# w_in's middle columns loaded in row halves of 512 columns, with eight blocks of the first tile computed in two halves

## The chip, the cores and the metric

The kernel runs on one core of a Trainium2 chip. A core has TensorE (PE, matrix products), VectorE (DVE), ScalarE (ACT), GpSimd (POOL) and the SyncE queue (SP), each with its own instruction stream; they wait for each other through semaphores. SP and POOL also issue DMAs. The metric is the device time of one execution in microseconds, lower is better. The time before is 282.33 us (median of 3 runs, 281.98 to 282.49).

## The reference, cut to what matters

Linear attention feeds a two-layer network with a snake activation.

```python
q_s = softmax over head_dim of q           # (8, 8, 576, 64)
k_s = softmax over the sequence of k
kv  = einsum('bhsd,bhse->bhde', k_s, v)
x   = einsum('bhsd,bhde->bhse', q_s, kv)   # reshaped to (4608, 512)
h   = x @ w_in                             # w_in: 512 x 2048, float32
s   = sin(alpha * h)
g   = h + s * s / (alpha + 1e-9)
out = g @ w_out                            # w_out: 2048 x 512
```

## The kernel before, in words

The 4608 tokens are cut into nine tiles of 512. For each tile the 2048 columns of h are cut into 16 blocks of 128. One block of one tile is a sum of four matmuls (`mm_h`, L275), one for each chunk of 128 rows of w_in, in the order `KO = (0, 2, 1, 3)` of chunks; `mm_h(t, ni, k0, k1)` does only the steps k0 to k1 of the four, so that a block can be begun at one place and finished at another. Steps 0 and 1 read chunks 0 and 2 of w_in and of x, steps 2 and 3 chunks 1 and 3.

A block ni of tile t then goes through `sine` (L286): ScalarE takes sin(alpha * h) from PSUM into a buffer s (four buffers), and s is squared on VectorE (D), POOL (P) or ScalarE (A) by a string of letters; for tile 0 it is `"DPPAPPAPPAAPPAPD"`. `combine` (L297) on VectorE adds h, still in PSUM, to the scaled square, and writes g. Only with that is the PSUM bank free. Which bank a block of tile 0 gets is written out (L266): `0: "aabbkllaabbkllaa"`, where a, b and l have two banks each and k (tile name kvp) has one. So block 11 takes the bank of block 4, blocks 7 and 8 those of 0 and 1, 9 and 10 those of 2 and 3, 12 and 13 those of 5 and 6.

The order of every engine's instructions is written out by hand. Tile 0 (L415 to L483): while the attention of batch 0 gives x in two steps (chunks 0 and 2 first, then 1 and 3), blocks 0 to 3 get their first two steps (L421, L428). Then `h_slot` (L431) runs for ni = 0 to 15: `mm_h` (from step 2 for the first four blocks, from step 0 for the others), then the sine, then the combine of the block before. Between them stand, in `late` (L476): after block 6 and after block 12 a copy on VectorE that lets SP load parts of q, k and v of batch 1, and after blocks 8 and 10 POOL's issues of w_out's rows 8 to 13. POOL's stand in its queue behind the squares of the blocks before them.

After tile 0 `o_quad` (L439) computes the output product of tile 0 in four accumulators at once, in the banks b, b, l, l (L485): first w_out's row blocks 0 to 3, then 4 to 7, 8 to 11 and 12 to 15. Between its steps stands the attention of batch 1 (L515 to L552): exponentials on ScalarE, sums and norm on VectorE, transposes and products on TensorE. From then on the tiles follow one another, h of one tile interleaved with the output product of the tile before.

w_in and w_out are float32 in DRAM and bf16 on the chip. The loads cast, and POOL issues them (L358 to L365): the columns 0 to 511 in three transfers by chunks, then four pieces of 256 columns with all four chunks (128x4x256, rows of 512 bytes on the chip), then the last quarter, columns 1536 to 2047, in one transfer (rows of 1024 bytes), then w_out's row blocks 0 to 3 and 4 to 7. SP's loads of q, k and v share the same 16 DMA engines.

Of the kernel before, what the change touches and what calls it, by code (L numbers as in the profile page):

```python
# [23 lines left out]
def kernel(  # L24
# [82 lines left out]
    def load_win(c0, c1, cc=slice(0, 4)):  # L107
        nc.gpsimd.dma_start(out=win[:, cc, c0:c1], in_=win_v[:, cc, c0:c1])  # L108
# [159 lines left out]
    def bank(kind):  # L268

        if kind == "k":  # L270
            return ps_k.tile([128, 2, MF], F32, name="kvp", tag="a")[:, 0]
        pool = {"a": lambda: ps_h[0], "b": lambda: ps_h[1], "l": lambda: ps_l, "o": lambda: ps_o[0], "p": lambda: ps_o[1]}[kind]()
        return pool.tile([128, MF], F32, name={"l": "lp", "o": "op", "p": "op"}.get(kind, "hp"), tag=kind)

    def mm_h(t, ni, k0=0, k1=4):  # L275

        if ni == 0 and k0 == 0:
            G[t] = gpool.tile([128, nN, MF], BF16, name="g")
        hp = HP[t, ni] if k0 else bank(BANKS.get(t, 3 * "aabb" + "abba")[ni])
        HP[t, ni] = hp  # L280
        for k in range(k0, k1):
            nc.tensor.matmul(hp, win[:, KO[k], ni * 128:(ni + 1) * 128],  # L282
                             xT[:, KO[k], t * MF % NX:t * MF % NX + MF], start=(k == 0), stop=(k == 3))
        return hp

    def sine(t, ni, hp, sq):  # L286
        s = spool.tile([128, MF], F32, name="s")
        nc.scalar.activation(s, hp, AX.Sin, scale=alpha_sb[:, ni:ni + 1])  # L288
        if sq == "A":
            nc.scalar.activation(s, s, AX.Square)  # L290
        elif sq == "P":
            nc.gpsimd.tensor_tensor(s, s, s, op=ALU.mult)  # L292
        else:
            nc.vector.tensor_tensor(s, s, s, op=ALU.mult)
        return s
# [62 lines left out]
    for c in range(2):  # L358
        load_win(256 * c, 256 * c + 256, slice(0, 4, 2))
    load_win(0, 512, slice(1, 4, 2))  # L360
    for c in range(2, 6):
        load_win(256 * c, 256 * c + 256)
    load_win(1536, 2048)
    for c in range(2):
        load_wout(4 * c, 4 * c + 4)  # L365
# [63 lines left out]
        mm_h(0, ni, ki, ki + 1)  # L429

    def h_slot(t, ni, sq, lag):  # L431
        hp = mm_h(t, ni, 2 if ni < (4, 2, 0)[min(t, 2)] else 0)
        lag.append((t, ni, hp, sine(t, ni, hp, sq)))

    def flush(lag, keep):
        while len(lag) > keep:
            combine(*lag.pop(0))
# [21 lines left out]
    with ES:  # L459
        def load_q1(ii):  # L460
            if ii == 0:
                staged["q", 1] = stage.tile([128, 4, J, D], F32, name="st_q", tag="st")
            st = staged["q", 1]
            DVE_CP(st[:, ii, 0, 0:1], zero)
            nc.sync.dma_start(out=st[:, ii::2, 0:8].rearrange("p i j d -> p i (j d)"),
                              in_=src_view(q, 1)[:, ii::2, 0:8 * D])

        def load_kv1():
            for n in "kv":
                staged[n, 1] = stage.tile([128, 4, J, D], F32, name=f"st_{n}", tag="st")  # L470
            for n, t, ii, j0, j1 in (("k", k, 0, 0, J), ("v", v, 0, 0, J), ("k", k, 1, 0, J),
                                     ("v", v, 1, 0, 5), ("v", v, 1, 5, J)):
                nc.sync.dma_start(out=staged[n, 1][:, ii::2, j0:j1].rearrange("p i j d -> p i (j d)"),
                                  in_=src_view(t, 1)[:, ii::2, j0 * D:j1 * D])

        late = {6: lambda: load_q1(0), 8: lambda: load_wout(8, 12), 10: lambda: load_wout(12, 14),  # L476
                12: lambda: (load_q1(1), load_kv1())}
        for ni in range(nN):
            h_slot(0, ni, "DPPAPPAPPAAPPAPD"[ni], lag)
            flush(lag, 1)  # L480
            if ni in late:
                late[ni]()
# [95 lines left out]
        for ni in range(nN):  # L578
            h_slot(1, ni, SQ[ni], lag)
            flush(lag, 1)  # L580
            if ni == 6:
                scale_q8()
            late_q8(ni)
# [69 lines left out]
    for ni in range(nN):  # L653
        h_slot(2, ni, SQ2[ni], lag)
        flush(lag, 2)
        if ni == 5:
            attn_kv(3)
        elif ni in (9, 13):
            ii = ni // 12
            x_copy(DVE_CP, slice(ii, 4, 2), 3, x_pair(3, ii))  # L660
    flush(lag, 0)

    for t in range(3, nT):
# [11 lines left out]
        for ni in range(nN):  # L675
            hp = mm_h(t, ni)
# [62 lines left out]
```

## Time and profile before

| what | us |
|---|---|
| median of 3 runs | 282.33 (281.98 to 282.49) |
| the profiled execution | 283.14 |
| its span | 281.3 |
| TensorE busy | 268.4 (95%) |
| ScalarE busy | 224.2 (80%) |
| VectorE busy | 187.1 (67%) |
| POOL busy | 80.2 (28%) |
| TensorE's mean granted clock, share of full | 0.999 |

Times in the profile are microseconds from the span's start. A matmul of 512 columns shows as 379 ns, but the next one starts before it ends, so TensorE's progress is read from the starts. The transfers of w_in landed at these times, read from the issue's start and the time to landing: columns 0 to 511 at 12.63, 13.30 and 15.53, the four pieces at 17.24, 18.52, 19.85 and 21.19, the last quarter at 24.50; w_out's row blocks 0 to 3 at 27.31, 4 to 7 at 31.07, 8 to 11 at 35.35, 12 and 13 at 38.29. Of batch 1, q landed at 29.78 and 34.91, and the parts of k and v at 37.73, 39.39, 40.83, 41.72 and 42.40.

### The profile page before, as it was taken

Reading aid. Unit: us, or ns where it says so; the run is one execution under the profiler, and the core shown is the slowest. Engines: PE = TensorE matmul, PEld = TensorE weight load, DVE = VectorE, ACT = ScalarE, POOL = GpSimd, SP = SyncE. Lnnn points to the kernel's source line nnn. Section 1 sums busy time; section 2 is a strip of 40 time slices with the busy share of each in tenths; the row PEclk is TensorE's granted clock in tenths of the full one; section 3 lists DMA queues with packets and bytes.
Section 4 is the critical chain, followed back from the end, with each engine's and each line's share of the span. In section 5 each row is a group of like instructions: output and inputs, shape, how many; then the busy total and the mean of one; then the engine's idle time right before and its main releaser. Section 6 shows DMA issues by size and latency. Waiting matters only on the chain.

```text
span 281.3 us, 4775 instructions
## 1 busy us (share of the span) xinstructions
PE 268.4 (95%) x1814; PEld 124.2 (44%) x1843; DVE 187.1 (67%) x279; ACT 224.2 (80%) x321; POOL 80.2 (28%) x75
## 2 busy tenths in 40 slices
PE   3899999999999999999999999999999999999994
PEld 1434454444444444444444444444444444444443
DVE  2968867999878767766776677577775555555422
ACT  4799457999588999899989998999877777777400
POOL 2959112678667450215011500350000000000000
PEclk9999999999999999999999999999999999999999
DMA  7999999795699039811981199125011111111143
GB/s 258 299 185 224 276 385 401 266 356 198 156 245 379 3 76 294 336 37 43 328 332 37 40 267 384 37 51 123 10 30 37 37 40 37 38 42 44 41 100 75
DMA packets 39607, 46.06 MB, mean 164 GB/s; under 512 B 17040, under 2 KB 22944, under 8 KB 39584
## 3 DMA queue, kind: packets, MB, share of 16 engines
q1 hardware_dynamic: 33952, 41.11, 46.1%
q0 software_dynamic: 5472, 4.52, 9.8%
q8 instruction: 14, 0.23, 0.3%
q10 hardware_dynamic: 160, 0.13, 0.2%
q14 instruction: 9, 0.07, 0.1%
HBM read 36.71 MB, written 9.44 MB: 164 GB/s over the span
## 4 chain that ended last, share of the span: by engine, by line
PE 87%; DMA 8%; POOL 2%; issue 1%; ACT 0%; SPq 0%; DVE 0%
PE hp L282 38%; PE op L302 37%; DMA wout<-in_moe_w_out_dram 4%; PE hp L302 2%; DMA win<-in_moe_w_in_dram 2%; PE lp L282 2%; DMA st_k<-in_k_dram 2%; PE kvp L173 2%; PE lp L302 1%; PE op L282 1%; PE op L709 1%; PE hp L237 1%; POOL s L292 1%; PE xp L237 1%; PE kvp L282 1%
## 5 line engine op out<-in xcount | busy, mean ns | idle before, releaser
L298 DVE SCALAR_TENSOR_TENSOR g<-s,inva_sb,hp 128x512 bf16<-128x512 f32 x129 | 95.1, 745 | 58.9 <-ACT s L290 53.3
L282 PE MATMUL hp<-xT,win 128*128 128x512 bf16 x508 | 128.8, 379 | 0.8 <-DMA win<-in_moe_w_in_dram 0.4
L302 PE MATMUL op<-wout,g 128*128 128x512 bf16 x463 | 117.6, 379 | 1.7 <-issue 1.3
L288 ACT ACTIVATE s<-hp,alpha_sb 128x512 f32<-128x512 f32 x129 | 87.0, 684 | 21.8 <-PE hp L282 20.3
L282 PEld LDWEIGHTS <-win 128*128 128x128 bf16 x576 | 55.6, 98 | 68.4 <-DMA win<-in_moe_w_in_dram 1.8
L302 PEld LDWEIGHTS <-g 128*128 128x128 bf16 x560 | 53.4, 98 | 65.4 <-issue 2.9
L290 ACT ACTIVATE s<-s 128x512 f32<-128x512 f32 x112 | 70.7, 632 | 3.6
L292 POOL TENSOR_TENSOR s<-s 128x512 f32<-128x512 f32 x28 | 29.5, 1066 | 17.8 <-ACT s L288 17.7
L152 POOL TENSOR_TENSOR qn<-qe,qs 128x1152 bf16<-128x1152 bf16 x11 | 23.2, 2128 | 30.7 <-DVE qs L146 26.3
L314 DVE COPY o<-op 128x512 f32<-128x512 f32 (+2 forms) x32 | 21.1, 660 | 9.7 <-PE op L302 7.4
L137 POOL CAST vb<-st_v 128x1152 bf16<-128x1152 f32 x12 | 14.4, 1228 | 44.5 <-DMA st_v<-in_v_dram 44.2
L118 ACT ACTIVATE qe<-st_q 128x1152 bf16<-128x1152 f32 (+2 forms) x18 | 17.7, 1026 | 6.3 <-DMA st_q<-in_q_dram 6.1
L118 ACT ACTIVATE ke<-st_k 128x1152 bf16<-128x1152 f32 x16 | 17.9, 1153 | 2.6 <-DMA st_k<-in_k_dram 2.6
L145 DVE TENSOR_REDUCE qs<-qe 128x36 f32<-128x2304 bf16 x5 | 12.8, 2552 | 8.3 <-ACT qe L118 8.3
L302 PE MATMUL hp<-wout,g 128*128 128x512 bf16 x45 | 12.0, 379 | 0.5 <-DMA wout<-in_moe_w_out_dram 0.3
L118 ACT ACT_TABLE_LOAD x7 | 9.0, 1283 | 0.8 <-PEq L723 0.7
L302 PE MATMUL lp<-wout,g 128*128 128x512 bf16 x32 | 9.2, 379 | 0.1
L369 PE MATMUL warm<-st_q,ident 128*128 128x512 f32 (+1 forms) x6 | 4.1, 806 | 4.7 <-DMA st_q<-in_q_dram 4.7
L282 PE MATMUL lp<-xT,win 128*128 128x512 bf16 x32 | 7.7, 379 | 0.4 <-DMA win<-in_moe_w_in_dram 0.4
L250 DVE CAST xT<-xp 128x1024 bf16<-128x1024 f32 (+1 forms) x7 | 7.4, 1065 | 0.0
L298 DVE SCALAR_TENSOR_TENSOR g<-s,inva_sb,lp 128x512 bf16<-128x512 f32 x8 | 5.7, 739 | 0.4 <-POOL s L292 0.4
L108 POOL DMA_DIRECT2D win<-in_moe_w_in_dram x8 | 5.9, 772 | 0.0
(98 smaller groups left out, 137.2 us busy)
## 6 DMA issues: line engine op xcount, KB each, us to landing
out_dram<-o SPq DMA_DIRECT2D x70, 128.0 KB, 2.3
st_q<-in_q_dram SPq DMA_DIRECT2D x6, 1152.0 KB, 6.3
st_k<-in_k_dram SPq DMA_DIRECT2D x6, 1152.0 KB, 9.1
st_v<-in_v_dram SPq DMA_DIRECT2D x6, 1152.0 KB, 11.3
st_k<-in_k_dram SPq DMA_DIRECT2D x4, 576.0 KB, 8.3
st_q<-in_q_dram SPq DMA_DIRECT2D x4, 512.0 KB, 6.2
wout<-in_moe_w_out_dram POOLq DMA_DIRECT2D x3, 512.0 KB, 13.7
win<-in_moe_w_in_dram POOLq DMA_DIRECT2D x5, 256.0 KB, 7.9
```

Source lines behind the costliest of these rows:

```text
L118: nc.scalar.activation(dst[:, :, ii * 128:(ii + 1) * 128].rearrange("p j (x d) -> p x j d", x=2), src[:, ii::2], AX.Exp)
L137: engs[ii](vv[:, 2 * ii:2 * ii + 2, :, 0:D], staged["v", b][:, ii::2])
L145: nc.vector.tensor_reduce(qs, A["qe", b].rearrange("p j (i d) -> p j i d", i=4), axis=AXL.X, op=ALU.add)
L152: engs[ii % len(engs)].tensor_tensor(qn[:, ii, 0:j1].rearrange("p j (x d) -> p j x d", x=2), qe[:, ii], part.unsqueeze(3).to_broadcast([12 ...
L250: eng(xT[:, c, d0:d0 + m - n], xp[..., n:m])
L282: nc.tensor.matmul(hp, win[:, KO[k], ni * 128:(ni + 1) * 128], xT[:, KO[k], t * MF % NX:t * MF % NX + MF], start=(k == 0), stop=(k == 3))
L288: nc.scalar.activation(s, hp, AX.Sin, scale=alpha_sb[:, ni:ni + 1])
L290: nc.scalar.activation(s, s, AX.Square)
L292: nc.gpsimd.tensor_tensor(s, s, s, op=ALU.mult)
L298: nc.vector.scalar_tensor_tensor(G[t][:, ni], in0=s, scalar=inva_sb[:, ni:ni + 1], in1=hp, op0=ALU.mult, op1=ALU.add)
L302: nc.tensor.matmul(acc, G[t][:, ni, j * 128:(j + 1) * 128], wout[:, ni, :], start=(ni == 0), stop=(ni == nN - 1))
L314: eng(o[:, cols], acc)
```

## The change

Columns 512 to 1535 of w_in come in four transfers as before, but each brings 512 columns of two chunks: first chunks 0 and 2 of columns 512 to 1023, then chunks 1 and 3 of them, then the same for columns 1024 to 1535. Rows on the chip are 1024 bytes per transfer instead of 512. In tile 0, ahead of block 4 the first two steps of blocks 4 to 7 are done, and ahead of block 8 those of blocks 8 to 11; `h_slot` then does only steps 2 and 3 of the blocks 4 to 11. Everything else stays in its order: on TensorE only these matmuls change places, POOL has four DMA issues of another shape, the other engines have the same instructions in the same order.

```diff
-    for c in range(2, 6):
-        load_win(256 * c, 256 * c + 256)
+    for c in (512, 1024):
+        for r in range(2):
+            load_win(c, c + 512, slice(r, 4, 2))
     load_win(1536, 2048)
...
     def h_slot(t, ni, sq, lag):
-        hp = mm_h(t, ni, 2 if ni < (4, 2, 0)[min(t, 2)] else 0)
+        hp = mm_h(t, ni, 2 if ni < (12, 2, 0)[min(t, 2)] else 0)
         lag.append((t, ni, hp, sine(t, ni, hp, sq)))
...
         for ni in range(nN):
+            for n in range(ni, ni + 4) if ni in (4, 8) else ():
+                mm_h(0, n, 0, 2)
             h_slot(0, ni, "DPPAPPAPPAAPPAPD"[ni], lag)
```

## The prediction

> **What bounds the kernel now.** I read the chain that ended last first, in order of time, because the change lies in the first tenth of the span and only the chain tells whether that tenth decides the end.
>
> ```profile
> 9.20 6.33 DMA win<-in_moe_w_in_dram
> 15.53 0.05 issue
> 15.57 1.90 PE hp L282 x8
> 17.48 0.86 PE kvp L282 x4
> 18.34 1.73 PE lp L282 x8
> 20.07 1.74 PE hp L282 x8
> 21.81 0.68 ACT s L288
> 22.56 1.98 POOL s L292 x2
> 24.54 10.81 DMA wout<-in_moe_w_out_dram
> 35.39 0.38 PE hp L302
> ```
>
> Columns: start, length, what. PE waits for w_in until 15.53, then two engines (ACT, POOL) lead to the issue of w_out's rows 8 to 11, which land at 35.35; from 35.39 on the chain is TensorE with issue gaps, to the end. So whatever moves TensorE's position at 35.39 moves the end one for one, as long as nothing later becomes late. Next, TensorE's timeline (start, length, what, idle before and its releaser):
>
> ```profile
> 15.57 1.90 PE L282 MATMUL hp<-xT,win 128*128 128x512 bf16 x8 [0.36 <-DMA win<-in_moe_w_in_dram]
> 17.31 1.03 PE L282 MATMUL kvp<-xT,win 128*128 128x512 bf16 x4
> 19.90 3.62 PE L282 MATMUL hp<-xT,win 128*128 128x512 bf16 x16
> 24.55 1.90 PE L282 MATMUL lp<-xT,win 128*128 128x512 bf16 x8 [0.39 <-DMA win<-in_moe_w_in_dram]
> 28.02 1.89 PE L302 MATMUL hp<-wout,g 128*128 128x512 bf16 x8
> 29.74 1.89 PE L302 MATMUL lp<-wout,g 128*128 128x512 bf16 x8
> 35.39 0.38 PE L302 MATMUL hp<-wout,g 128*128 128x512 bf16 x1 [0.30 <-DMA wout<-in_moe_w_out_dram]
> ```
>
> One matmul starts every 0.216 us ((3.62 - 0.38)/15). Between 15.57 and 35.39 TensorE stands twice: 0.39 before block 12 (w_in's last quarter) and 0.30 for w_out, 0.69 in all. That is the most that this change can win. The pieces of 256 columns are never waited for beyond hundredths: block 4 starts at 17.31.
>
> The ScalarE timeline in the same stretch shows no gap over 0.04 us between 16.28 and 29.10, 12.8 us for 16 sines (0.57 from one to the next) and 5 squares; so a late sine there is never made up. Last, the transfers: the software queue alone, first in the 512-byte packets of the pieces (17 to 19 us), then in the 1024-byte packets of the last quarter and w_out (21.2 to 24).
>
> ```profile
> DMA packets 787, 0.39 MB, mean 195 GB/s; under 512 B 25, under 2 KB 787, under 8 KB 787
> ...
> DMA packets 570, 0.57 MB, mean 203 GB/s; under 512 B 15, under 2 KB 570, under 8 KB 570
> ```
>
> **The change, part by part.**
>
> *POOL's issues.* Four transfers of 256 KB become four of 256 KB. The issue of the 128x2x512 shape took 0.74 (L108 at 9.20), that of 128x4x256 0.79: 4 x 0.05 = 0.2 us earlier for the last quarter and w_out's first halves. Both wait in the queue for some 10 us before they land, and POOL's next work is at 17.63 after an idle 2.48. Worth nothing.
>
> *The transfers.* 1,048,576 bytes at 195 GB/s are 5.38 us, at 203 GB/s 5.17. So the four land about 1.29 apart, at 17.2, 18.5, 19.8 and 21.1, the last quarter at 24.3 (24.50 before), w_out 8 to 11 at 35.15 (35.35). Bounds for the interval: 1.28 (18.52 - 17.24, the shortest of the pieces) below; above, 1.65 (the last quarter, 24.50 - 21.19 = 3.31 for 512 KB) and, farthest, 2.23 (15.53 - 13.30: the one earlier transfer of exactly this shape). I take 1.29, because the packet rate holds over all engines, and the two slow ones have a cause of their own: at 20.5 to 21.3 a 16 KB instruction fetch shares the queues, and from 12.6 to 15.2, when that earlier transfer ran, the queue moved only 153 GB/s with packets of both sizes in it.
>
> A rule speaks against it. The Trainium skill, "DMA: Bandwidth & Descriptors", section "Why a DMA increments its semaphore by 16 and not by 1", says that a transfer has landed only when all 16 engines have reported. Section "Latency and other measured facts" adds that some engines are usually slower than the rest, and guesses at the software queue's descriptor rings. By it the interval would be the slowest engine's 1.65; the first rival works this out from rows.
>
> *The order on TensorE.* The same 32 matmuls and weight loads, no new instruction. From 17.31: first halves of blocks 4 to 7 (8 x 0.216), second halves from 19.03 (their half of w_in lands at 18.5: no wait), first halves of 8 to 11 from 20.77 (19.8), second halves after. What it costs is when a block is complete, since its sine waits for that. Block 4: second half at 19.03 and 19.25, complete 19.63; before 18.34.
>
> *The chain behind it.* Sine 4 began at 19.27 because ScalarE was busy; now at 19.68 (+0.41). Its square on POOL goes from 20.02 to 20.43 and its combine on VectorE ends at 22.25 instead of 21.85. That frees the bank kvp, which block 11 uses. Block 11's first half is now due at 22.06 (17.31 + 22 x 0.216) and not at 23.36, so TensorE waits 0.25, a new wait; second halves of 8 to 11 queue behind it. Block 8's second half starts at 22.74, it is complete at 23.34, and sine 8 starts at 23.39 instead of 22.38: +1.0. As ScalarE has no gap from there, all sines to the last are 1.0 later (29.10 becomes 30.1), and with them the combines: block 12's ends at 30.05 instead of 29.03.
>
> *TensorE to 35.39.* Block 12 starts after 32 matmuls and the wait: 17.31 + 32 x 0.216 + 0.25 = 24.47, after the landing at 24.3: 0.08 earlier than 24.55. The first output matmul comes at 27.92 (28.02). The third accumulator uses block 12's bank (lp, 29.74 before, when the bank had been free since 29.03). Now TensorE arrives at 29.63 and the bank comes free at 30.05, with 0.06 to react 30.11: a wait of 0.48. The eight matmuls later for the fourth accumulator arrive at 30.97, its bank is free at 30.7. So w_out's rows 8 are reached at 34.92 - 0.10 + 0.48 = 35.30; they have landed at 35.15. The wait of 0.30 is gone, in its place stand the two bank waits. TensorE passes at 35.30 instead of 35.39: **-0.1 us**.
>
> *POOL and the queues behind it.* POOL's issue of w_out 8 to 13 stands behind the square of block 8: 24.54 becomes 25.2. It costs nothing while w_out 4 to 7 are in front of it until 31.07. SP's loads of batch 1 wait for two VectorE copies (22.76 and 27.94) that move by 0.4 and 1.0. The second set is issued at 29.1 instead of 28.11. The DMA share is 0.96 or more in every stretch from 15.5 to 60 us, so what q1 does not take, w_out takes: the last of these loads should land where it did (42.40), less 0.2. The first of them, q of batch 1 (landed 34.91), may be 1.0 later: exp at 36.0, sums and norm on VectorE end at 39.85 (38.85), and TensorE transposes them at 39.93. Cover 0.08, nearly used up. Bounds for this step: 0, and +0.9 if the loads of v keep the delay of 1.0 (v is cast 42.42 to 42.85 and used at about 43.0).
>
> Sum: span 281.3 - 0.1 = 281.2. The profiled execution took 283.14, with 1.84 around its span, so it would be 283.04; it lies 0.81 above the median of the three runs, 282.33. Against that median: 282.2.
>
> **The rivals.** A measurement of this kernel tells about 0.2% (0.56 us) from no change.
>
> *Row halves land slowly (slower).* Place: w_in's columns 512 to 1535. Price: if the slowest engine needs 1.65 for each 256 KB of 1024-byte packets, as the last quarter's 3.31 says, the four land at 17.2, 18.8, 20.5 and 22.1, the last quarter at 25.4, w_out at 36.3; TensorE passes at 36.33, +0.94: 283.3. With 2.23 it is w_out at 38.6, +3.25: 285.6. It decides from an interval of 1.48 on. For it: the only two measured landings of 1024-byte transfers next to this place. Against: 203 GB/s, and w_out's first half, 2.81 for 512 KB, 1.40 each.
>
> *The delayed sines reach batch 1 (slower).* Place: the copy at 27.94 that lets SP load. Price: up to +0.75 (1.0 later loads less a cover of some 0.25 before the v product): 283.1. For it: the transposes' cover is 0.08. Against: the DMA engines are full, so order changes and not the end.
>
> *The waits go and none comes (faster).* If sine 8 is late by no more than 0.6, the banks are free in time, TensorE passes as soon as w_out lands; with 0.69 of waits gone 281.6 at best. For it: w_out can land up to 0.5 earlier, as its queue keeps the engines alone for 1.0 us longer. Against: the bank of block 12.
>
> **How the numbers follow.** As worked out (own range 282.0 to 282.7): 0.53. Slow landing 0.24, batch 1 0.12, faster 0.11. All of the first lies within 0.2%, the next two are slower, the last faster: slower 0.36, same 0.53, faster 0.11. The range from 281.7 to 283.4 takes in the faster case's larger part, all of the forecast, and both slower cases up to the 1.65 interval; outside are the 2.23 one and the best of the faster one.
>
> **What would show it.** Right: landings about 1.3 apart, no wait for w_in's last quarter, a wait of about 0.25 before kvp's block 11 and of about 0.5 before the third accumulator, ScalarE's last sine of tile 0 ending near 30.1, and no wait for w_out at 35.3. Wrong: landings over 1.48 apart; TensorE waiting for w_in at block 8 or 12; a gap before the transposes of batch 1 or before its second v product.

## The result, and the profile after

The changed kernel takes 283.2 us (median of 15 runs, 282.48 to 284.33) against 282.33 for the kernel before (median of 15, 281.7 to 282.91): a ratio of 1.0034, 95% interval 1.0023 to 1.0046. It is slower by about 0.9 us, where the prediction had it 0.1 faster. One later execution of the changed kernel took 1613 us, with its matmuls 1.32 us apart (six times as far as usual) at a granted clock that reads 1.00 in its profile; the cause is not known, and no ratio, count or distance below contains it.

The profiles seem to say the opposite. The profiled execution of the changed kernel took 282.87 with a span of 281.1; that of the kernel before 283.14 with 281.3. The first was below the median of its kernel, the second 0.8 above its own. So the two traces can't simply be subtracted, and that is the heart of this case.

The changed kernel's chain that ended last, in order of time (start, length, what; pieces called issue, under 0.1 us each, are left out here and in the other chains below):

```profile
16.95 0.70 DVE s L294
17.68 0.76 DVE g L298
18.48 0.59 PE hp L282 x2
...
19.54 0.70 ACT s L288
20.30 1.05 POOL s L292
21.38 0.76 DVE g L298
22.18 0.59 PE kvp L282 x2
...
23.24 0.70 ACT s L288
24.00 1.05 POOL s L292
25.08 0.76 DVE g L298
...
26.32 0.68 ACT s L288
27.08 2.04 POOL s L292 x2
29.14 0.76 DVE g L298
29.94 1.89 PE lp L302 x8
```

Where the chain before went through the landings of w_in and w_out, it now runs from sine to square to combine to TensorE and round again: no transfer stands in this stretch. TensorE's timeline of the same execution (start, length, what, idle before and its releaser; kvp is the bank k, lp the banks l, hp the banks a and b):

```profile
17.38 1.03 PE L282 MATMUL lp<-xT,win 128*128 128x512 bf16 x4
18.48 0.59 PE L282 MATMUL hp<-xT,win 128*128 128x512 bf16 x2
...
20.20 1.89 PE L282 MATMUL hp<-xT,win 128*128 128x512 bf16 x8
22.18 0.59 PE L282 MATMUL kvp<-xT,win 128*128 128x512 bf16 x2
...
27.79 1.89 PE L302 MATMUL hp<-wout,g 128*128 128x512 bf16 x8
29.94 1.89 PE L302 MATMUL lp<-wout,g 128*128 128x512 bf16 x8 [0.26 <-DVE g L298]
...
35.12 0.59 PE L302 MATMUL hp<-wout,g 128*128 128x512 bf16 x2
```

At one start every 0.216 us, the matmul after the four from 17.38 was due at 18.24 and began at 18.48; the one after the eight from 20.20 was due at 21.93 and began at 22.18; the one after the eight from 27.79 was due at 29.52 and began at 29.94. Three waits for a bank: 0.24 (block 7, for block 0's), 0.25 (block 11, for block 4's) and 0.42 (third accumulator, for block 12's), 0.9 in all. The idle column shows less, since a matmul is drawn as 379 ns. At 35.12 TensorE takes up w_out's row block 8, which had landed at 33.36; its matmuls were held up by no transfer after 13.04.

### The profile page after: what moved, and what is told of

The parts are those of the page before. It is cut to its first block, busy times and chain, and to the rows that moved or that the text cites. A ratio compares the mean times of both kernels' runs of the same rounds, so it can differ in the third digit from the quotient of the medians.

```text
span 281.1 us, 4804 instructions
## 1 busy us (share of the span) xinstructions
PE 271.1 (96%) x1843; PEld 124.4 (44%) x1843; DVE 187.1 (67%) x279; ACT 223.8 (80%) x321; POOL 80.9 (29%) x75
## 4 chain that ended last, share of the span: by engine, by line
PE 89%; DMA 4%; POOL 2%; ACT 2%; DVE 1%; issue 1%; SPq 0%; ACTq 0%
PE hp L282 37%; PE op L302 37%; PE hp L302 3%; PE lp L302 3%; DMA win<-in_moe_w_in_dram 2%; DMA st_k<-in_k_dram 2%; PE kvp L173 2%; POOL s L292 1%; PE op L282 1%; PE op L712 1%; PE lp L282 1%; DVE g L298 1%; ACT s L288 1%; PE hp L237 1%; PE kvp L282 1%; PE xp L237 1%
## 5 line engine op out<-in xcount | busy, mean ns | idle before, releaser
L302 PE MATMUL op<-wout,g 128*128 128x512 bf16 x480 | 120.4, 379 | 0.0
L302 PE MATMUL hp<-wout,g 128*128 128x512 bf16 x48 | 12.7, 380 | 0.0
```

Of the source, the lines that this page charges most:

```text
L302: nc.tensor.matmul(acc, G[t][:, ni, j * 128:(j + 1) * 128], wout[:, ni, :], start=(ni == 0), stop=(ni == nN - 1))
```

## The experiments

In every trace I measure two distances: from the start of tile 0's first sine to the matmul with w_out's row block 8 (35.39 in the trace before, 35.12 in the one above), and from there to the end of the span. The second is the same within 0.4 us in all traces (245.93 to 246.33), so the first carries most of the result; what the 0.4 is comes up behind the experiments with fewer blocks. "Distance" below is the first one. The three theories: *banks* (late sines hold banks that TensorE waits for), *transfers* (the row halves land late), *batch 1* (its q is loaded later, because a VectorE copy behind the sines lets SP issue it).

**One part of the change alone.** Row halves with whole blocks (the edit against the changed kernel, as in all diffs of this section but the last):

```diff
-        hp = mm_h(t, ni, 2 if ni < (12, 2, 0)[min(t, 2)] else 0)
+        hp = mm_h(t, ni, 2 if ni < (4, 2, 0)[min(t, 2)] else 0)
...
-            for n in range(ni, ni + 4) if ni in (4, 8) else ():
-                mm_h(0, n, 0, 2)
```

> Row halves for w_in's columns 512 to 1535, but every block computed whole, as before. Bank theory (the loss comes from late sines, which hold PSUM banks that TensorE then waits for): block 4 waits for its second row half, 0.8 us, while the sines keep their times, since ScalarE is busy to 19.2; the wait before w_in's last quarter shrinks, no bank wait; +0.1 to +0.5 over the kernel before. Transfer theory (1024-byte row halves land late in many executions): as slow as the changed kernel or slower, +0.9 or more, and as widely spread. Batch 1 theory (q of batch 1 is loaded later because a copy behind the sines lets it go): the copy moves by at most 0.4, so +0.5 at most.

Measured: 282.61 against 282.15, ratio 1.0015 (1.0002 to 1.0029), spread 282.35 to 283.29. TensorE's timeline:

```profile
17.24 0.59 PE L282 MATMUL kvp<-xT,win 128*128 128x512 bf16 x2
18.25 0.61 PE L282 MATMUL kvp<-xT,win 128*128 128x512 bf16 x2 [0.41 <-DMA win<-in_moe_w_in_dram]
```

The second half of block 4 was due at 17.67 and waits 0.58 for its row half (0.8 expected); there is no bank wait, and the distance is 18.54. The +0.46 lies in the banks theory's range; the batch 1 theory allowed up to 0.5 too, and the transfers theory wanted 0.9 or more.

The other part alone, the pieces of 256 columns with the blocks in halves:

```diff
-    for c in (512, 1024):
-        for r in range(2):
-            load_win(c, c + 512, slice(r, 4, 2))
+    for c in range(2, 6):
+        load_win(256 * c, 256 * c + 256)
```

> The four pieces of 256 columns as before, with blocks 4 to 11 in two halves as in the change. Bank theory: the same bank waits as in the changed kernel (0.25 at block 11, about 0.45 at the third accumulator) and one more for the piece with block 6, 0.4; +0.9 to +1.2 over the kernel before. Transfer theory: the pieces land as before, so no more than the one wait for a piece, +0.2 to +0.4. Batch 1 theory: the copy is as late as in the changed kernel, +0.9.

Measured: 282.79 against 282.15, ratio 1.0023 (1.0011 to 1.0034), distance 18.88. The third accumulator waits as in the changed kernel:

```profile
27.50 1.89 PE L302 MATMUL hp<-wout,g 128*128 128x512 bf16 x8
29.66 1.89 PE L302 MATMUL lp<-wout,g 128*128 128x512 bf16 x8 [0.27 <-DVE g L298]
```

Block 11 waits 0.25 as well. The third wait is another one: block 6 waits 0.22 for its piece of 256 columns, and block 7 behind it then finds block 0's bank free. So the order of the blocks alone brings a loss of the same size; the new transfers are not needed for it. The +0.64 is under the +0.9 to +1.2 that I expected.

**Fewer blocks in halves.** Only blocks 4 to 7:

```diff
-        hp = mm_h(t, ni, 2 if ni < (12, 2, 0)[min(t, 2)] else 0)
+        hp = mm_h(t, ni, 2 if ni < (8, 2, 0)[min(t, 2)] else 0)
...
-            for n in range(ni, ni + 4) if ni in (4, 8) else ():
+            for n in range(ni, ni + 4) if ni == 4 else ():
```

> Row halves, blocks 4 to 7 in two halves, blocks 8 to 11 whole. Bank theory: block 11 no longer asks early for block 4's bank, sine 8 is late by 0.2 instead of 0.9, the wait at the third accumulator is 0.1 or none; -0.2 to +0.2 against the kernel before. Transfer theory: as the changed kernel, +0.9. Batch 1 theory: the copy is only 0.3 late, so -0.2 to +0.3 too; this run does not tell it from the bank theory.

Measured: 282.17 against 282.15, ratio 1.0012 (0.9986 to 1.0038; one run of 285.63 widens it), distance 18.28. The same with block 11 alone taken out of the second group:

```diff
-        hp = mm_h(t, ni, 2 if ni < (12, 2, 0)[min(t, 2)] else 0)
+        hp = mm_h(t, ni, 2 if ni < (11, 2, 0)[min(t, 2)] else 0)
...
-            for n in range(ni, ni + 4) if ni in (4, 8) else ():
+            for n in range(ni, min(ni + 4, 11)) if ni in (4, 8) else ():
```

> The changed kernel, but block 11 is computed whole in its own place; blocks 4 to 10 stay in two halves. Bank theory: only block 11 asks for block 4's bank early, so the wait of 0.25 there goes, sine 8 starts about 22.6 instead of 23.24 and the third accumulator waits 0.1 or less: 0.5 to 0.7 under the changed kernel, -0.1 to +0.2 against the kernel before. Transfer theory and batch 1 theory: as the changed kernel, +0.7 or more.

Measured: 282.19 against 282.32, ratio 1.0005 (0.9992 to 1.0018), distance 18.27. TensorE's timeline:

```profile
19.86 3.19 PE L282 MATMUL hp<-xT,win 128*128 128x512 bf16 x14
22.88 0.81 PE L282 MATMUL kvp<-xT,win 128*128 128x512 bf16 x3
...
27.20 1.89 PE L302 MATMUL hp<-wout,g 128*128 128x512 bf16 x8
29.00 1.89 PE L302 MATMUL lp<-wout,g 128*128 128x512 bf16 x8
```

Fourteen matmuls follow one another from 19.86, block 11 comes at 22.88 without a wait, and the third accumulator, due at 28.93, waits 0.07 in place of 0.42. One block moved takes 0.60 of the 0.90 away (the 0.90 is 18.87 less the 17.97 of the kernel before without a wait, which comes further down); the row halves are all still there. Last, only blocks 4 to 6, so that block 7 does not ask early for block 0's bank either:

```diff
-        hp = mm_h(t, ni, 2 if ni < (12, 2, 0)[min(t, 2)] else 0)
+        hp = mm_h(t, ni, 2 if ni < (7, 2, 0)[min(t, 2)] else 0)
...
-            for n in range(ni, ni + 4) if ni in (4, 8) else ():
+            for n in range(ni, ni + 3) if ni == 4 else ():
```

> Row halves, only blocks 4 to 6 in two halves, 7 to 11 whole. Bank theory: block 7 does not ask early for block 0's bank either (0.2), sines as in the kernel before, no bank wait: -0.1 to -0.4 against the kernel before, the best of these versions. Transfer theory: +0.7 or more, like the changed kernel.

Measured: 282.28 against 282.32, ratio 1.0001 (0.9982 to 1.002), distance 18.30. No bank wait is left, but this execution waits 0.20 for w_in's last quarter and 0.13 for w_out's row block 8. Expected was a gain; there is none that can be measured. No version that I ran beats the kernel before.

The traces show a second limit behind the first. Without block 11, the chain that ended last comes neither from banks nor from w_out, but from batch 1's v:

```profile
29.99 10.92 DMA st_v<-in_v_dram
40.96 0.74 POOL vb L501
41.75 0.71 PE kvp L184 x18
```

The same stands in the trace with only blocks 4 to 7 in halves (v at 40.90) and in one of the kernel before (the third one below, v at 40.73). In these three the second distance is 246.19 to 246.33; in the traces of the changed kernel, which comes later and finds v there, it is 245.95 or 245.96. So of what TensorE gains by an earlier arrival at row block 8, 0.2 to 0.4 can be lost again, and a difference of the first distance need not show in full in the time.

**Batch 1's loads one block earlier**, in the changed kernel:

```diff
-                12: lambda: (load_q1(1), load_kv1())}
+                11: lambda: (load_q1(1), load_kv1())}
```

> The changed kernel, with the copy that lets SP load the rest of batch 1 behind block 11 instead of block 12 on VectorE, 1.6 us earlier than in the changed kernel and before its place in the kernel before. Bank theory: all bank waits stay, +0.7 to +0.9 over the kernel before, like the changed kernel. Batch 1 theory: the slower executions of the changed kernel (283.2 to 284.3) go and the time is near 282.5, +0.2. Transfer theory: as the changed kernel, +0.9.

Measured: 283.27 against 282.15 (4 runs, 282.71 to 283.82), ratio 1.0044 (1.0027 to 1.0061), distance 19.14. q of batch 1 landed at 33.66 instead of 35.58, and nothing was won. In exchange w_out's row blocks 8 to 11 landed at 34.92, later than the 33.36 above, and TensorE waited 0.27 for them. With q earlier nothing got faster, and in the changed kernel's traces the second distance has no wait for batch 1 in it: the batch 1 theory falls.

**The two kernels once more, for other executions.**

> The kernel before once more, for the trace of another execution; its first trace was of an execution 0.8 us above the median. Bank theory: w_in's columns 0 to 511 land by 15.0 (15.53 in the first trace) and w_out 8 to 11 before TensorE asks for it, so that only the 0.3 before w_in's last quarter is left of the waits, and the output product reaches w_out 8 to 11 near 34.5, 0.65 before the changed kernel. Transfer theory: the same waits as in the first trace, about 0.7, and 35.4.

> The changed kernel once more, for its spread and the trace of another execution. Bank theory: none of its times below 282.4, +0.2 to +0.4% over the kernel before, bank waits of 0.25 at block 11 and 0.2 to 0.5 at the third accumulator in the trace whatever the landings. If the trace is of an execution above 283.2, its extra time is looked for in the landings of w_in and w_out. Transfer theory: the low times of the kernel before (281.7) are reached in some executions.

The kernel before, in an execution of 281.73 with a span of 279.9, 1.4 less than the span of its first trace. TensorE's timeline:

```profile
16.63 1.03 PE L282 MATMUL kvp<-xT,win 128*128 128x512 bf16 x4
17.49 1.89 PE L282 MATMUL lp<-xT,win 128*128 128x512 bf16 x8
19.22 3.62 PE L282 MATMUL hp<-xT,win 128*128 128x512 bf16 x16
...
23.54 1.89 PE L282 MATMUL lp<-xT,win 128*128 128x512 bf16 x8
25.26 1.89 PE L282 MATMUL hp<-xT,win 128*128 128x512 bf16 x8
26.99 1.89 PE L302 MATMUL hp<-wout,g 128*128 128x512 bf16 x8
28.72 1.89 PE L302 MATMUL lp<-wout,g 128*128 128x512 bf16 x8
...
33.90 0.38 PE L302 MATMUL hp<-wout,g 128*128 128x512 bf16 x1
```

No matmul of this stretch waits: w_in's columns 0 to 511 landed at 14.45 (15.53 in the first trace), the last quarter at 23.28 (24.50), w_out 8 to 11 at 33.34 (35.35). All three waits that the prediction read from the first trace are absent, also the one for w_in's last quarter, which I expected to stay. The distance is 17.97; in the first trace it was 19.11. A third trace agrees:

> The kernel before, for the trace of a third execution: from the first sine to w_out's rows 8 to 11 about 17.97 us where the transfers are in time, more by TensorE's waits for transfers where they are not, and no bank wait in either case.

Measured: 281.97 in the profiled execution, distance 17.97 again, no wait over 0.06 up to that point. Both executions lie below the median of the kernel before over all its comparison runs (282.24), by 0.51 and 0.27; none at the median itself was traced, so how much of the first trace's waits the median execution has is not shown.

The changed kernel again took 282.71 against 282.32 (ratio 1.0020, 0.9999 to 1.0041); its trace is of no use here. None of its executions is below 282.42, where the transfers theory wanted some near 281.7, the kernel before's lowest.

**What the changed kernel's longest executions lose.** Its times reach 284.85. Three more sets of executions, of which the first has its trace from such a one:

> The changed kernel, for the trace of an execution above 283.2. Bank theory plus late landings: the two bank waits (0.25 and about 0.45) as always, and the rest of its time over 282.5 is TensorE waiting for a transfer (w_in's columns 0 to 511, w_in's last quarter, w_out's rows 8 to 11, or the loads of batch 1), which the kernel before shows in its slow executions too. Batch 1 theory: the rest stands before the transposes of batch 1's q or its v product.

> As the run before it: another execution of the changed kernel, to see where those above 283.2 lose more than the bank waits. Same two expectations.

> As the two before it: another execution of the changed kernel. Same two expectations.

Measured: 283.59, 282.57 and 283.36 against 282.14 (ratios 1.0049, 1.0014 and 1.0047). The profiled execution of the first took 284.29. Its chain, from the start:

```profile
7.33 6.25 DMA st_v<-in_v_dram
13.61 0.44 DVE vb L352
14.09 0.40 PE kvp L184 x8
...
17.78 0.59 ACT s L288
```

A part of batch 0's v landed at 13.59 (11.47 in the changed kernel's first trace), so the first sine came at 17.69 instead of 16.25. From there everything is as before, only later: the distance is 18.86. The third trace (283.25) starts at 16.64 with 18.87, the changed kernel's first trace at 16.25 with 18.87. So what these two lose over it lies ahead of the first sine. The bank waits are the same 0.9 in each, and there is no wait at batch 1's transposes. The second trace (282.63) is different: it has 19.03, with three waits for w_in (0.27, 0.11 and 0.15) and bank waits of only 0.25 at block 11 and 0.26 at the third accumulator. While transfers held TensorE up there, the banks had more time to come free. My expectation named other transfers; it was v of batch 0.

**A later start.** One VectorE memset of 128x1024 between the two halves of a cast of batch 0's v, in the kernel before, in the changed one and in the one without block 11 (the same lines in each):

```diff
+    pad = singles.tile([128, 1024], F32, name="pad")
...
     cast_v0(1, 0, 5, DVE_CP)
+    nc.vector.memset(pad, 0.0)
     cast_v0(1, 5, 9, DVE_CP)
```

> The kernel before with one VectorE memset of 128x1024 float32 more, ahead of the second half of batch 0's v cast (L352): it makes the first sine later by its length, about 1.0, as late loads of batch 0 do in the changed kernel's slow executions. If the kernel before hides a late start (its waits for transfers shrink): +0.3 to +0.6 over the kernel before. If a late start passes through one for one: +0.9 to +1.1.

> The changed kernel with the same memset. With the bank waits between the first sine and w_out's rows 8 to 11 fixed, a late start passes in full: lowest time 283.3 to 283.5, against 282.4 for the changed kernel, +1.7 to +2.0 over the median of the kernel before.

> Blocks 4 to 10 in two halves, block 11 whole, with the same memset. As the first of these three: +0.3 to +0.6 over the kernel before if a late start is hidden, +0.9 to +1.1 if it passes.

| with the memset | median | lowest, and without it | ratio to the kernel before | first sine | distance |
|---|---|---|---|---|---|
| kernel before | 282.48 | 282.36, 281.61 | 1.0008 (0.9996 to 1.0019) | 16.86 | 17.97 |
| changed | 283.26 | 283.23, 282.36 | 1.0038 (1.0023 to 1.0053) | 16.70 | 18.86 |
| without block 11 | 282.72 | 282.57, 281.75 | 1.0022 (1.0007 to 1.0037) | 16.69 | 18.27 |

The distances move by no more than 0.01, while the first sine is 0.78 to 0.93 later than the earliest one traced without the memset (for the changed kernel, whose start varies from 15.87 to 17.69, this is the second of its three later traces). In the lowest times the memset shows with 0.75 to 0.87. In the medians it nearly disappears: +0.09 for the kernel before, under both of my expectations, and +0.87 in place of +1.7 to +2.0 for the changed one (its lowest, 283.23, is just under the 283.3 to 283.5 expected). A likely reading, not shown by a trace of such an execution, is that most executions already lose up to 0.8 in waits ahead of or beside the tile, and that a later start hides those. The three kernels with nearly the same start differ by what the distances say: 282.36, 282.57 and 283.23 in the lowest times, that is 0.21 and 0.87 for 0.30 and 0.89.

**What stays open.** Of 48 executions of the changed kernel 13 lie more than 1.5 us above its lowest, 283.9 or more; of 117 of the kernel before (all its comparison runs) 5 lie that far above theirs, 283.12 or more. The one such execution that was traced lost its time to v of batch 0, which is issued ahead of every transfer that the change touches. Why this should come more often in the changed kernel no run shows. It is not needed for the direction of the result: the lowest times differ by 0.75 and the medians of all those runs by 0.61 (282.24 and 282.855). Both are less than the 0.90 of the distances; batch 1's v and the transfer waits that some executions of the kernel before have work that way, but how much each takes is not measured.

## Why the prediction was wrong

*POOL's issues* and *the order on TensorE* came as written: the four issues show as 0.77 to 0.79 each and start 0.71 to 0.72 apart (0.74 foretold), the matmuls stand in the order foretold, nothing behind the issues is late.

*The transfers* came as forecast in the changed kernel's first trace: the four landed at 16.84, 18.09, 19.37 and 20.64, 1.25 to 1.28 apart (1.29 foretold). The Trainium skill ("DMA: Bandwidth & Descriptors", section "Latency and other measured facts") says that some DMA engines are usually slower than the others; no interval of 1.65, which the prediction put beside this from rows, came between the row halves in this trace. The last quarter took 3.31 for 512 KB again (23.95 - 20.64), as in the first trace of the kernel before, but 1.89 to 3.82 in the other traces, so it is no fixed rate. And in one of the changed kernel's traces, the one with 19.03, the fourth row half landed 3.03 after the third (19.30 and 22.33). An instruction fetch stands in that stretch; whether it is the cause is not shown. It cost TensorE the 0.11 named above.

*The chain behind it* was right in kind and nearly in size. ScalarE's timeline in the changed kernel:

```profile
18.68 0.63 ACT L290 ACTIVATE s<-s 128x512 f32<-128x512 f32 x1
19.54 0.69 ACT L288 ACTIVATE s<-kvp,alpha_sb 128x512 f32<-128x512 f32 x1 [0.23 <-PE kvp L282]
...
23.24 1.27 ACT L288 ACTIVATE s<-hp,alpha_sb 128x512 f32<-128x512 f32 x2 [0.62 <-PE hp L282]
```

Sine 4 waits 0.23 and sine 8 0.62 for their blocks. Counted from the first sine, sine 8 comes at 6.99 (6.10 before): 0.89 late, foretold 1.0. Block 11's wait is 0.25 (0.25 foretold), the third accumulator's 0.42 (0.48 foretold). Not named was block 7's 0.24 for block 0's bank. In the first trace TensorE reached block 4 only at 17.31; here it is there at 16.95 and asks before the bank is free.

*The step that failed is "TensorE to 35.39"*: "The wait of 0.30 is gone, in its place stand the two bank waits", with the sum of -0.1. Set against the first trace it was not far off: 18.87 from the first sine, where that trace has 19.11. But the term on the other side, the waits of the kernel before, was read from one execution and taken for all. It was 19.11 there and is 17.97 in the later traces, 1.14 less, with no wait in it. Against those the bank waits cost +0.90: the two foretold, 0.25 and 0.48, would have made +0.73; measured were 0.25 and 0.42, and block 7's 0.24, which the prediction put at nothing. The prediction had the sign of this in hand: the profiled execution lay 0.81 above the median, and it carried that 0.81 over as a constant instead of asking whether it was the very waits that it used (0.39 and 0.30 as what can be won, and 0.36 in the 17.31 from which it counted).

*The rivals*: none of the three explains the loss. Slow landing happened to one row half in one trace and cost 0.11; the loss is there without it. Batch 1: q did land later (35.58 for 34.91) and VectorE's norm ended at 39.52, 0.31 ahead of the transposes at 39.83; moving the loads up won nothing. The faster case needed sine 8 less than 0.6 late. The rival that happened was missing: the same bank waits as forecast, in an execution where nothing was there to be won.

## What to carry to other kernels

Before a wait in a trace is counted as gain, ask whether other executions have it: if the profiled execution lies above the median by about what the waits sum up to, they may be that execution's own, and a second trace tells. Starting several blocks early in halves asks for their PSUM banks sooner and makes each of them complete later. Both cost here: the first 0.24 and 0.25 at blocks 7 and 11, the second, through block 8's late sine, 0.42 at the third accumulator. One block of eight (the one with the single bank) had two thirds of the price. Distances between two fixed instructions compare executions better than whole spans.

## What the runs showed of the hardware that I had not expected

- From the first sine to w_out's row block 8 the same kernel takes the same time to 0.01 us in executions whose spans differ by 0.8 to 1.4 us (17.97 three times, 18.86 or 18.87 four times, the memset runs included), and more only in the two traces where matmuls wait for transfers (19.11 and 19.03). In these traces the variation comes from transfers and the start, not from the engines.
- A 256 KB load of v landed 2.1 us later in one execution than in another (13.59 and 11.47), with the engines in the same order; one of its 4096-byte packets is recorded with 2.31 us.
